# Attention rewritten as two passes over the scores, with two heads on the two halves of the TensorE array

## The chip, the cores and the metric

The kernel runs on one core of one Trainium2 chip. The metric is device time in microseconds (us) for one execution; lower is better. The program is one launch with three stages: causal attention with a learned decay, a first feed-forward of 2048 hidden units, and a second, gated feed-forward of 1536 hidden units.

## The reference

```python
B, H, S, D = 4, 8, 576, 64
scores = (1.0 / np.sqrt(D)) * np.matmul(q, k.transpose(0, 1, 3, 2))
causal = np.triu(np.ones((S, S), dtype=bool), k=1)
cum = np.cumsum(np.maximum(s, 0.0), axis=-1)
bias = -(cum[:, :, :, None] - cum[:, :, None, :])
scores = np.where(causal, -1e9, scores + np.minimum(bias, 0.0))
scores = scores - np.max(scores, axis=-1, keepdims=True)
attn = np.exp(scores)
attn = attn / (np.sum(attn, axis=-1, keepdims=True) + 1e-09)
out = np.matmul(attn, v)
x = out.transpose(0, 2, 1, 3).reshape(B * S, H * D)      # 2304 tokens of 512
h = x @ w_in;  y = softplus(h) @ w_out                   # first feed-forward
xn = y / rms(y) * rms_g
out = (silu(xn @ w_gate) * (xn @ w_val)) @ w_out2        # second feed-forward
```

The weights arrive as 64-bit floats. A product of two numbers is formed from parts: `hi` is a number rounded to the short type fp32r, `lo` is what is left, and three products (hi·hi, hi·lo, lo·hi) are added up.

## The kernel before

**Attention.** The 32 heads are taken as 16 pairs of two heads of one batch. For a pair, `a_load` fetches q and k, `a_qt` transposes them on TensorE (PE, 12 transposes, L357), and `a_qh` and `a_ql` split them into `hl`, whose partitions 0 to 63 belong to the first head and 64 to 127 to the second. `a_qd` copies the parts of one head by DMA into a tile `sk` (L381, L382), so that one matmul contracts over 68 rows (four of them carry the bias) and a second over 128 rows (both mixed products stacked). `a_s` makes the scores with queries on partitions, in four blocks of 128, 256, 384 and 512 keys (L418, L419), and adds the causal mask by a bf16 product (L420). The last 64 queries of both heads share one tile (`a_s4`, L427 to L431). `a_m` takes the negative row maximum on VectorE (DVE, L436), `a_e` the exponential with that maximum as bias and the row sum as a by-product on ScalarE (ACT, L449), and `a_n` scales each row by one over its sum on GpSimd (POOL, L472). `a_t` transposes the result on PE, with 15 transposes for a head, ten of 128 rows (L504) and five of 64 (L501). Then `a_v0` multiplies the first 384 queries by v in full float32 (L530, 64 columns of weights), and `a_v1` the others from hi and lo parts (L539).

**What sets the order.** Every engine runs its own instructions in program order. In attention the table `OFF` gives each step of head n the place n + offset, and all steps are sorted by it. Twelve of the weight chunks are converted meanwhile (`CONV`, on ACT, DVE and POOL). SP issues all of these DMAs, one after another.

**After attention.** `m1_h` (L642 to L644) needs x, which attention has written to DRAM as `xT`. The first two of these, H0 and H1, are placed at the end of the attention order. ACT, DVE and POOL then turn h into `gh` and `gl` (`m1_abs` to `m1_gl`; in the first six steps `m1_gl` runs on POOL, L694), and `m1_y` needs both. The tiles of this stage lie where the pools of attention lay, and wait for their last readers.

Of the kernel before, what the change touches and what calls it, by code (L numbers as in the profile page):

```python
# [8 lines left out]
F32 = mybir.dt.float32  # L9
# [131 lines left out]
def attention_moe_kernel(ctx, tc, q, k, v, s, w_in, w_out, w_gate, w_val, w_out2, rms_g, out):  # L141
    nc = tc.nc
# [46 lines left out]
    mask64 = const.tile([P, 64], BF16, tag="mask64", name="mask64")  # L189
    bds = []  # L190
    ones = const.tile([P, P], F32R, tag="ones", name="ones")
    gcol = const.tile([P, KD], F32, tag="gcol", name="gcol")
    aug = dram.tile([NH, 4, 2, S], F32R, tag="aug", name="aug")
    aug4 = dram.tile([NH, 4, P + S], F32R, tag="aug4", name="aug4")
# [92 lines left out]
    st = {}  # L287

    def setup():
# [3 lines left out]
        for r in (slice(0, 64), slice(64, P)):  # L293
            nc.gpsimd.tensor_copy(out=mask64[r], in_=mask16[r, r])
        for i in range(2):
            bd = pools["stack"].tile([P, 2, P], F32R, tag=f"bd{i}", name=f"bd{i}", bufs=1)
            bds.append(bd)
            nc.gpsimd.memset(f32(bd), 0.0)
        nc.vector.memset(f32(ones), 1.0)

    def make_cum(cp):
# [6 lines left out]
        rows = cp.tile([NH, 4, 2, S], F32R, tag="rows", name="rows")  # L308
        for r, w in ((0, 0), (1, 1), (2, 0), (3, 1)):
            nc.gpsimd.memset(f32(rows[:, r, w]), 1.0)  # L310
        zero = cp.tile([NH, 4, 64], F32, tag="zero", name="zero")
        nc.gpsimd.memset(zero, 0.0)
        for hd in range(2):
            c = (1 - hd) * 64
            nc.gpsimd.dma_start(out=f32(aug4[hd::2, :, c:c + 64]), in_=zero[hd::2])
# [3 lines left out]
        hi, lo = rows[:, 0, 1], rows[:, 2, 1]  # L319
        nc.vector.tensor_copy(out=hi, in_=cum)  # L320
        nc.scalar.activation(out=rows[:, 1, 0], in_=f32(hi), func=AF.Copy, scale=-1.0)
        nc.vector.tensor_tensor(out=lo, in0=cum, in1=f32(hi), op=ALU.subtract)
        nc.vector.tensor_tensor(out=rows[:, 3, 0], in0=f32(hi), in1=cum, op=ALU.subtract)
        nc.sync.dma_start(out=f32(aug), in_=f32(rows))
        for hd in range(2):
            nc.sync.dma_start(out=f32(aug4[hd::2, :, hd * 64:hd * 64 + 64]), in_=f32(rows[hd::2, :, 0, 512:S]))
        nc.sync.dma_start(out=f32(aug4[:, :, P:P + S]), in_=f32(rows[:, :, 1]))
        nc.gpsimd.dma_start(out=gcol, in_=rms_g.rearrange("(a p) -> p a", p=P))

    def pair_bh(p):  # L330
        return p // HP, 2 * (p % HP)

# [8 lines left out]
    def a_loadv(p):  # L341
        b, h = pair_bh(p)
        t = pools["nat"].tile([P, NB, 2, D], F32, tag="vn", name="vn", bufs=3)
        for hd in range(2):
            nc.sync.dma_start(
                out=t[:, 0:4, hd, :],
                in_=v[b, h + hd, 0:512, :].rearrange("(c p) d -> p c d", p=P))
        nc.sync.dma_start(
            out=t[:, 4], in_=v[b, h:h + 2, 448:576, :].rearrange("h p d -> p h d"))
        st["vn", p] = t  # L350

    def a_qt(p, which):
        nat = st.pop((("qn", "kn")[which], p))
        t = ps_s("qkT"), ps_s("qkT")
# [8 lines left out]
    def a_qh(p, which):  # L363
        if which == 0:
            st["hl", p] = pools["split"].tile([P, 4, S], F32R, tag="hl", name="hl", bufs=2)
# [10 lines left out]
    def a_qd(n):  # L376
        p, hd = divmod(n, 2)
        hl = f32(st["hl", p])[hd * D:(hd + 1) * D]
        sk = pools["stack"].tile([P, 2, 2, 512], F32R, tag="sk", name="sk", bufs=3)
        for dst, src in ((sk[4:4 + D, 0], hl[:, 0:3:2]), (sk[0:D, 1], hl[:, 0:4:3]), (sk[D:P, 1], hl[:, 1:3])):  # L380
            nc.sync.dma_start(out=f32(dst), in_=src[:, :, 0:512])  # L381
        nc.sync.dma_start(out=f32(sk[0:4, 0]), in_=f32(aug[n][:, :, 0:512]))  # L382
        st["sk", n] = sk

    def a_qb(p):
        a8 = pools["stack"].tile([8, P + S], F32R, tag="a8", name="a8", bufs=2)
        nc.sync.dma_start(out=f32(a8), in_=f32(aug4[2 * p:2 * p + 2]).rearrange("h r n -> (h r) n"))
# [11 lines left out]
    def a_vl(p):
        vn, vs = st["vn", p], st["vs", p]  # L400
        nc.gpsimd.tensor_tensor(out=vs[:, :, 1:3, :], in0=vn, in1=f32(vs[:, :, 0:4:3, :]), op=ALU.subtract)

    BLK = ((0, 2, 3), (1,))
    COL = {0: 0, 2: 1, 3: 2, 1: 3}
    SOFF = {0: 0, 1: 0, 2: 128, 3: 0}
    EO = {0: 0, 1: 128, 2: 384, 3: 768}

    def a_s(n, half):
        sk = st["sk", n]
        for blk in BLK[half]:  # L410
            if blk == 2:
                t = st["s", n, 0]
            else:
                t = st["x1"][:, 0:256] if blk == 1 else ps_s("s")
            st["s", n, blk] = t
            c, w = SOFF[blk], B0[blk] + P
            o, i = t[:, c:c + w], slice(B0[blk], w)
            nc.tensor.matmul(o, sk[0:D + 4, 0, 0, i], sk[0:D + 4, 0, 1, 0:w], start=True, stop=False)  # L418
            nc.tensor.matmul(o, sk[:, 1, 0, i], sk[:, 1, 1, 0:w], start=False, stop=False)  # L419
            nc.tensor.matmul(t[:, c + w - P:c + w], ident16, mask16, start=False, stop=True)  # L420

    def a_s4(p):
        a8, bd, hl = st.pop(("a8", p)), bds[p % 2], st["hl", p]
        t = st["s4", p] = ps_s("s4")[:, 0:256], ps_s("s4")[:, 0:320]
        for o, j0, w in ((t[0], 0, 256), (t[1], 256, 320)):
            j = slice(j0, j0 + w)
            nc.tensor.matmul(o, a8[:, 0:P], a8[:, P + j0:P + j0 + w], start=True, stop=False)  # L427
            nc.tensor.matmul(o, bd[:, 0], hl[:, 2, j], start=False, stop=False)
            nc.tensor.matmul(o, bd[:, 0], hl[:, 3, j], start=False, stop=False)
            nc.tensor.matmul(o, bd[:, 1], hl[:, 2, j], start=False, stop=(j0 == 0))  # L430
        nc.tensor.matmul(t[1][:, 256:320], ident16, mask64, start=False, stop=True)  # L431

    def a_m(n, blk):
        w = B0[blk] + P
        m = st["m", n, blk] = pools["sml"].tile([P, 1], F32, tag=f"m{blk}", name="m")
        nc.vector.reduce_max(out=m, in_=st["s", n, blk][:, SOFF[blk]:SOFF[blk] + w], axis=AX.X, negate=True)  # L436

    def a_m4(p):
        m = st["m4", p] = pools["sml"].tile([P, 2], F32, tag="m4", name="m4", bufs=2)
        for i, t in enumerate(st["s4", p]):  # L440
            nc.vector.reduce_max(out=m[:, i:i + 1], in_=t, axis=AX.X, negate=True)
        nc.vector.tensor_tensor(out=m[:, 0:1], in0=m[:, 0:1], in1=m[:, 1:2], op=ALU.min)

    def a_e(n, blk):
        if blk == 0:
            st["e", n] = pools["e"].tile([P, 1280], F32, tag="e", name="e")
            st["z", n] = pools["sml"].tile([P, 4], F32, tag="z", name="z")
        w, c = B0[blk] + P, COL[blk]
        nc.scalar.activation(out=st["e", n][:, EO[blk]:EO[blk] + w], in_=st["s", n, blk][:, SOFF[blk]:SOFF[blk] + w],  # L449
                             func=AF.Exp, bias=st.pop(("m", n, blk)), accum_out=st["z", n][:, c:c + 1])  # L450

    def a_e4(p):
        e = st["e4", p] = pools["e"].tile([P, S], F32, tag="e4", name="e4", bufs=2)
        z = st["z4", p] = pools["sml"].tile([P, 2], F32, tag="z4", name="z4", bufs=2)
        m = st.pop(("m4", p))
        for i, (t, c) in enumerate(zip(st.pop(("s4", p)), (slice(0, 256), slice(256, S)))):
            nc.scalar.activation(out=e[:, c], in_=t, func=AF.Exp, bias=m[:, 0:1], accum_out=z[:, i:i + 1])

    def a_r(n):
        r = st["r", n] = pools["sml"].tile([P, 4], F32, tag="r", name="r")  # L460
        z = st["z", n]
        nc.vector.tensor_scalar(out=z, in0=z, scalar1=1e-9, scalar2=None, op0=ALU.add)
        nc.vector.reciprocal(out=r, in_=z)

    def a_r4(p):
# [5 lines left out]
    def scale_rows(e, r):  # L471
        nc.gpsimd.tensor_scalar(out=e, in0=e, scalar1=r, scalar2=1.0, op0=ALU.mult, op1=ALU.mult)  # L472
# [484 lines left out]
```

## Time and profile before

| what | value |
|---|---|
| time, median of 2 runs | 1242.48 us (1240.45 to 1244.51) |
| the profiled execution, first to last instruction | 1242.4 us |
| PE busy | 1176.2 us (95%) |
| DVE, ACT, POOL busy | 771.7, 617.7, 471.5 us |
| first score matmul of attention | at 18.42 us |
| first h of the first feed-forward | at 314.62 us |
| first y of the first feed-forward | at 326.15 us |

A row of the timeline gives the start, the length, the engine, the line of the kernel, the operation, what it writes and reads, its shape, and how often it is repeated (x6); a bracket names idle time before it and what ended it. The length of a matmul includes its way through the array, so the pace of PE is read from the difference between the starts of neighbouring rows.

### The profile page before, as it was taken

How to read it: one execution, taken by the hardware profiler on the slowest of the kernel's cores; microseconds unless marked ns; L12 is line 12 of the kernel's file. 1: busy time of each engine (PE TensorE's matmuls, PEld its weight loads, DVE VectorE, ACT ScalarE, POOL GpSimd, SP SyncE). 2: the span in 40 equal slices, each digit the busy share in tenths (PEclk: the TensorE clock that was granted, in tenths of full speed). 3: DMA queues.
4: the chain of work that ended last, by engine and by line, in shares of the span. 5: the costliest groups of instructions: out<-in, count | busy, mean ns of one | idle time of the engine just before them, and what ended most of it. 6: DMA issues, size and time to landing. Idle time of an engine off the chain costs nothing.

```text
span 1242.4 us, 18308 instructions
## 1 busy us (share of the span) xinstructions
PE 1176.2 (95%) x6404; PEld 1042.1 (84%) x6404; DVE 771.7 (62%) x1396; ACT 617.7 (50%) x1467; POOL 471.5 (38%) x487
## 2 busy tenths in 40 slices
PE   4999999999999998999989879999999999999998
PEld 3677777776988888999888768899999999999997
DVE  4666676654699999998999999533333332333322
ACT  2667666665677777866666666442121121212111
POOL 4455655543354544346576776762000000000000
PEclk9999999999899998999999999999999999999999
DMA  9998888753333343544452332331101010010000
GB/s 181 198 192 178 200 193 186 167 131 100 99 129 119 122 139 123 162 140 134 159 165 91 120 101 85 117 97 58 39 14 39 14 39 1 14 39 13 26 1 26
DMA packets 139037, 128.96 MB, mean 104 GB/s; under 512 B 66656, under 2 KB 116352, under 8 KB 138912
## 3 DMA queue, kind: packets, MB, share of 16 engines
q1 hardware_dynamic: 138848, 127.74, 38.6%
q8 instruction: 51, 0.84, 0.3%
q14 instruction: 42, 0.34, 0.1%
q0 software_dynamic: 96, 0.04, 0.0%
HBM read 76.46 MB, written 26.12 MB: 83 GB/s over the span
## 4 chain that ended last, share of the span: by engine, by line
PE 67%; DVE 22%; ACT 4%; issue 3%; DMA 2%; SPq 2%; POOL 1%; DVEq 0%; POOLq 0%; ACTq 0%
DVE gl L694 5%; PE x L539 4%; PE pt L504 4%; PE g L644 4%; PE g L643 4%; PE v L644 4%; PE v L643 4%; PE v L642 4%; PE g L642 4%; PE o L530 4%; DVE l L685 4%; DVE e L677 3%; PE o L818 3%; PE o L819 3%; PE o L817 3%
## 5 line engine op out<-in xcount | busy, mean ns | idle before, releaser
L643 PE MATMUL y<-gl,w 128*128 128x384 f32 x384 | 134.5, 350 | 25.4 <-DVE gl L694 24.1
L252 POOL TENSOR_TENSOR wf<-ur 128x512 int32<-128x512 int32 x68 | 94.3, 1386 | 123.7 <-DVE ur L246 34.1
L802 DVE TENSOR_TENSOR u<-g,u 128x384 f32<-128x384 f32 x71 | 39.5, 556 | 158.9 <-ACT u L801 158.9
L642 PE MATMUL y<-gh,w 128*128 128x384 f32 x384 | 130.8, 341 | 3.1 <-ACT l L669 1.4
L644 PE MATMUL y<-gh,w 128*128 128x384 f32 x384 | 130.6, 340 | 0.0
L472 POOL TENSOR_SCALAR e<-e,r 128x256 f32<-128x256 f32 (+2 forms) x144 | 78.3, 560 | 127.9 <-ACT hl L368 103.1
L804 ACT ACTIVATE gh<-l 128x384 fp32r<-128x384 f32 x72 | 37.8, 524 | 156.0 <-DVE l L803 156.0
L801 ACT ACTIVATE u<-g 128x384 f32<-128x384 f32 x71 | 34.8, 490 | 151.9 <-PE g L644 151.8
L643 PEld LDWEIGHTS y<-gl,w 128*128 128x128 f32 x384 | 73.3, 191 | 36.7 <-DVE gl L694 35.1
L643 PE MATMUL g<-xl,w 128*128 128x384 f32 x284 | 95.6, 336 | 1.8 <-DVE xl L636 1.8
L689 ACT ACTIVATE gh<-l 128x384 fp32r<-128x384 f32 x96 | 49.9, 520 | 93.7 <-DVE l L685 93.5
L642 PE MATMUL g<-xh,w 128*128 128x384 f32 x284 | 95.8, 337 | 0.7 <-ACT xh L635 0.7
L694 DVE TENSOR_TENSOR gl<-l,gh 128x384 fp32r<-128x384 f32 x90 | 93.1, 1035 | 4.5 <-ACT gh L689 0.7
L644 PE MATMUL g<-xh,w 128*128 128x384 f32 x284 | 95.9, 338 | 0.0
L642 PE MATMUL h<-xh,w 128*128 128x384 f32 x256 | 89.2, 348 | 6.8 <-DVE e L681 6.6
L642 PE MATMUL v<-xh,w 128*128 128x384 f32 x284 | 94.9, 334 | 0.0
L644 PE MATMUL v<-xh,w 128*128 128x384 f32 x284 | 94.9, 334 | 0.0
L643 PE MATMUL v<-xl,w 128*128 128x384 f32 x284 | 94.9, 334 | 0.0
L643 PE MATMUL h<-xl,w 128*128 128x384 f32 x256 | 88.4, 345 | 3.5 <-POOL xl L639 3.3
L644 PE MATMUL h<-xh,w 128*128 128x384 f32 x256 | 87.4, 341 | 0.0
L685 DVE TENSOR_TENSOR l<-l,e 128x384 f32<-128x384 f32 x96 | 84.0, 875 | 3.7
L677 DVE SCALAR_TENSOR_TENSOR e<-u,e 128x384 f32<-128x384 f32 x96 | 73.9, 770 | 17.1 <-ACT l L669 17.1
(191 smaller groups left out, 3281.7 us busy)
## 6 DMA issues: line engine op xcount, KB each, us to landing
sk<-hl SPq DMA_DIRECT2D x96, 256.0 KB
raw<-in_moe_w_out_dram SPq DMA_DIRECT2D x28, 512.0 KB
raw<-in_moe_w_in_dram SPq DMA_DIRECT2D x16, 512.0 KB
raw<-in_moe_w_gate_dram SPq DMA_DIRECT2D x12, 512.0 KB
raw<-in_moe_w_val_dram SPq DMA_DIRECT2D x12, 512.0 KB
wf<-wf SPq DMA_DIRECT2D x24, 256.0 KB
wl<-wf SPq DMA_DIRECT2D x24, 256.0 KB
xr<-x SPq DMA_DIRECT2D x28, 192.0 KB
```

The lines of the kernel that those rows point to most:

```text
L252: nc.gpsimd.tensor_tensor(out=w.bitcast(I32), in0=u, in1=r3, op=ALU.add)
L472: nc.gpsimd.tensor_scalar(out=e, in0=e, scalar1=r, scalar2=1.0, op0=ALU.mult, op1=ALU.mult)
L504: nc.tensor.transpose(t[:, o:o + P], e[:, EO[ib] + j0:EO[ib] + j0 + P], ident)
L530: nc.tensor.matmul(o[:, IS - w:IS], vn[:, jb, hd, :], x[:, c:c + w], start=(jb == 0), stop=(jb == 2))
L539: nc.tensor.matmul(t[:, 192 - w:192], vs[r, jb, 2 * hd:2 * hd + 2, :].rearrange("p a d -> p (a d)"), x[r, c:c + w], start=(i == 0 and jb = ...
L642: nc.tensor.matmul(o, wh, xh, start=start, stop=False)
L643: nc.tensor.matmul(o, wh, xl, start=False, stop=False)
L644: nc.tensor.matmul(o, wl, xh, start=False, stop=stop)
L677: nc.vector.scalar_tensor_tensor(out=e, in0=st.pop(("u", i)), scalar=-1.0, in1=e, op0=ALU.add, op1=ALU.subtract)
L685: nc.vector.tensor_tensor(out=l, in0=l, in1=st.pop(("e", i)), op=ALU.add)
L689: nc.scalar.activation(out=gh, in_=st["l", i], func=AF.Copy)
L694: eng.tensor_tensor(out=gl, in0=st.pop(("l", i)), in1=f32(st["gh", i]), op=ALU.subtract)
```

## The change

Attention is rewritten; the feed-forward stages keep their code.

- **Pass one** (`a_one`) makes the scores of a pair from the hi parts alone, queries on partitions. For each block there are two matmuls a head: one over 40 rows (`aq` and `all`, which hold the bias rows of eight pairs, with `a_aq` picking one pair's), one over the 64 rows of `hl`. The heads alternate: the first uses partitions 0 to 63, the second 64 to 127, each with its own PSUM bank. The copies into `sk` are gone.
- `a_m` takes the row maxima (DVE), `a_mt` transposes them (PE), `a_mh` rounds them (ACT), and `a_md` sends them by four DMAs as a further row into `aq`.
- **Pass two** (`a_two`) makes the scores again, with keys on partitions and from all parts, four matmuls for each block and head; the maximum is subtracted inside the product. `a_e` takes the exponential. No transposes of it follow.
- `a_v` multiplies by `vn`, which has a block of ones between the two heads' values, in full float32 with 128 columns of weights: 64 rows of the result are the values, 64 the row sums.
- The sum goes by DMA into a tile of 9 columns (`a_zd`), is inverted (`a_zr`), goes to DRAM (`a_rd`) and back, spread over 64 partitions (`a_rb`); `a_xm` multiplies on POOL, `a_xw` writes x.
- The order is made by `attention_order`, which gives each step an engine, a duration, what it waits for and a priority, and takes the step that can start first.

The diff, cut to its core (PSUM tags: four banks `s`, two `p`, one each `o0` and `x1`):

```diff
+        for i in range(3):
+            t = pools["nat"].tile([P, NB, 3, D], F32, tag=f"vn{i}", name=f"vn{i}", bufs=1)
+            nc.gpsimd.memset(t[:, :, 1, :], 1.0)
+            nc.gpsimd.memset(t[0:64, 4], 0.0)
+        for g in range(2):
+            for w in range(2):
+                t = pools["stack"].tile([P, S], F32R, tag=f"all{g}{w}", name=f"all{g}{w}", bufs=1)
+                for r in (slice(32, 64), slice(96, P)):
+                    nc.gpsimd.memset(f32(t[r]), float(w))
...
+    ONE = {
+        "A": ((0, 0, 0, 128, 1), (128, 256, 0, 384, 1)),
+        "B": ((0, 384, 0, 512, 1),),
+        "C": ((0, 128, 0, 256, 1), (256, 448, 320, 256, 1)),
+        "D": ((0, 448, 0, 320, 0),),
+    }
+    TWO = {
+        "a": ((0, 0, 0, 448, 128),),
+        "b": ((0, 0, 448, 128, 0), (128, 384, 384, 192, 128), (320, 448, 512, 64, 64)),
+        "c": ((0, 128, 128, 448, 128),),
+        "d": ((0, 256, 256, 320, 128),),
+    }
+    def a_one(p, banks, last):
...
+                for a in range(2):
+                    for hd in range(2):
...
+                        if a == 0:
+                            r = slice(64 * hd, 64 * hd + MR)
+                            x, y = aq[r, ii], al[r, jj]
+                        else:
+                            x, y = hl[r, 0, ii], hl[r, 2, jj]
+                        nc.tensor.matmul(t[hd][:, c:c + w], x, y, start=(n == 0 and a == 0),
...
+                nc.tensor.matmul(t[hd][:, c:c + P], ident16, mask16, start=False, stop=True, skip_group_check=True)
+    def a_md(p):
...
+            nc.sync.dma_start(out=aq[r, 0:512], in_=mt[4 * hd:4 * hd + 4])
+            nc.sync.dma_start(out=aq[r, 512:S], in_=mt[8 + hd:9 + hd, 64:P])
+    def a_two(p, banks, last):
...
+                for a, (x, y) in enumerate(((None, None), (2, 0), (2, 1), (3, 0))):
+                    for hd in range(2):
...
+    def a_v(p, hd, part):
...
+            jobs = ((0, 0, 0, 384), (1, 832, 128, 256), (2, 1280, 256, 128))
...
+            jobs = ((0, 384, 0, 192), (3, 576, 0, 192), (4, 768, 128, 64), (1, 1088, 0, 192), (2, 1408, 0, 192))
+        for n, (jb, c, oc, w) in enumerate(jobs):
+            nc.tensor.matmul(o[:, oc:oc + w], vn[:, jb, hd:hd + 2].rearrange("p a d -> p (a d)"), e[:, c:c + w],
...
+    def a_zd(p):
+            nc.sync.dma_start(out=z[half(hd)], in_=st["xz", p, hd][64 - 64 * hd:65 - 64 * hd, :])
+    def a_rd(p):
+        nc.sync.dma_start(out=rdd[p].rearrange("h (p c) -> (h p) c", c=9), in_=st.pop(("z", p)))
+    def a_rb(p):
+            nc.sync.dma_start(out=rb[half(hd)], in_=rdd[p][hd:hd + 1].broadcast_to([64, S]))
+    def a_xm(p):
+            nc.gpsimd.tensor_tensor(out=x[r], in0=st.pop(("xz", p, hd))[r], in1=rb[r], op=ALU.mult)
...
```

PE, in the middle of attention. Before, one head's larger score blocks (`s`), a mask, and the transposes of an earlier head's rows (`pt`):

```order
L418 MATMUL s<-sk 128x384
L419 MATMUL s<-sk 128x384
L420 LDWEIGHTS ident_76
L420 MATMUL s<-mask_77,ident_76 128x128
L418 MATMUL s<-sk 128x512
L419 MATMUL s<-sk 128x512
L420 LDWEIGHTS ident_76
L420 MATMUL s<-mask_77,ident_76 128x128
L504 MATMUL pt<-ident,e 128x128 x6
```

Now, at such a place, the last block of pass one (`s`) and the first two banks of pass two of another pair (`t`); x2 is one matmul for each head, x6 three:

```order
L434 MATMUL s<-all_162,aq 128x320 x2
L434 MATMUL s<-hl 128x320 x2
L492 MATMUL t<-aq,all_162 128x448 x2
L492 MATMUL t<-hl 128x448 x6
L492 MATMUL t<-aq,all_162 128x128 x2
L492 MATMUL t<-hl 128x128 x6
L492 MATMUL t<-aq,all_162 128x192 x2
L492 MATMUL t<-hl 128x192 x6
L492 MATMUL t<-aq,all_162 128x64 x2
L492 MATMUL t<-hl 128x64 x6
L499 LDWEIGHTS mask_77
L499 MATMUL t<-ident_76,mask_77 128x128
```

The transposes are gone, and runs of half-height matmuls of the two heads stand in the place of full-height ones; the masks come together behind them.

POOL, at the start of the program. Before, between the masks and the bias rows (`rows`):

```order
L294 COPY mask64_78<-mask16_77 64x64 x2
L298 MEMSET bd0_133 128x256
L298 MEMSET bd1_135 128x256
L310 MEMSET rows_154 32x576 x4
```

Now, at that place, after two rows each for `vn0` and `vn1` that read like those for `vn2`:

```order
L302 MEMSET vn2_150 128x5x64
L303 MEMSET vn2_150 64x192
L309 MEMSET all00_153 32x576 x2
L309 MEMSET all01_156 32x576 x2
L309 MEMSET all10_159 32x576 x2
L309 MEMSET all11_162 32x576 x2
L313 MEMSET mc0_165 128x128
L313 MEMSET mc1_167 128x128
L329 MEMSET rows_190 32x576 x4
```

The filling of `vn`, `all` and `mc` has come ahead of `rows`, which the first bias DMAs wait for.

POOL, at the end of attention, now; `x<-xz,rb` is `a_xm`, two for each pair, and `gl` the first feed-forward's:

```order
L399 TENSOR_SCALAR aq<-all_159,oh 128x576
L551 TENSOR_TENSOR x<-xz,rb 64x576 x10
L769 TENSOR_TENSOR gl<-l,gh 128x384
L714 TENSOR_TENSOR xl<-xr,xh 128x384
L769 TENSOR_TENSOR gl<-l,gh 128x384
```

The last pair's multiplication by its inverted sums stands ahead of the first `gl`.

## Rows read from the trace of the kernel before

**Rows 1.** The span, from the page of the profile.
```profile
span 1242.4 us, 18308 instructions
```

**Rows 2.** A stretch of attention by engine: busy us (instructions), granted clock, DMA share, GB/s.
```profile
120.00:160.00 40.00, 40.00 (x246) 28.42 (x244) 28.26 (x78) 26.95 (x85) 20.58 (x29) 1.00 0.84 194
```

**Rows 3.** PE's timeline, from one pair's first score matmul to the next pair's.
```profile
154.14 0.33 PE L418 MATMUL s<-sk 68*128 68x128 f32 x1
...
155.26 0.40 PE L419 MATMUL s<-sk 128*128 128x512 f32 x1
155.50 0.23 PE L420 MATMUL s<-mask,ident 128*128 128x128 bf16 x1
155.57 0.83 PE L504 MATMUL pt<-ident,e 128*128 128x128 f32 x6
156.15 0.36 PE L418 MATMUL x<-sk 68*128 68x256 f32 x1
...
156.54 0.67 PE L357 MATMUL qkT<-ident,qn 96*128 96x96 f32 x6
157.05 0.27 PE L504 MATMUL pt<-ident,e 128*128 128x128 f32 x1
157.25 0.27 PE L501 MATMUL pt<-ident,e 64*128 64x64 f32 x1
157.45 0.33 PE L504 MATMUL pt<-ident,e 128*128 128x128 f32 x1
...
157.98 1.51 PE L530 MATMUL o<-p,vn 128*64 128x384 f32 x6
159.42 0.33 PE L504 MATMUL pt<-ident,e 128*128 128x128 f32 x1
...
165.06 0.28 PE L429 MATMUL s<-hl,bd 128*128 128x256 f32 x1
165.17 0.28 PE L430 MATMUL s<-hl,bd 128*128 128x256 f32 x1
...
165.97 0.31 PE L429 MATMUL s<-hl,bd 128*128 128x320 f32 x1
166.12 0.31 PE L430 MATMUL s<-hl,bd 128*128 128x320 f32 x1
...
171.82 0.33 PE L418 MATMUL s<-sk 68*128 68x128 f32 x1
```

**Rows 4.** Groups by line and shape, up to 400 us: busy us, mean ns of one.
```profile
L436 DVE TENSOR_REDUCE m<-s 128x1 f32<-128x512 f32 x32 | 21.8, 682 | 1.3 <-PE s L420 1.3
...
L401 POOL TENSOR_TENSOR vs<-vn,vs 128x640 fp32r<-128x640 f32 x16 | 24.7, 1546 | 1.3
```

**Rows 5.** The timeline of the start, all engines.
```profile
0.74 0.40 SPq L303 DMA_DIRECT2D sv<-in_s_dram  x1
...
2.67 0.53 DVE L316 TENSOR_SCALAR sv<-sv 32x576 f32<-32x576 f32 x1 [1.08 <-DMA sv<-in_s_dram]
...
3.65 2.45 POOL L310 MEMSET rows<- 32x576 f32 x4
...
14.25 1.39 SPq L382 DMA_DIRECT2D sk<-aug  x1
...
18.42 0.45 PE L418 MATMUL s<-sk 68*128 68x128 f32 x1 [8.58 <-DMA sk<-aug]
...
28.14 0.67 PE L418 MATMUL s<-sk 68*128 68x384 f32 x1
...
28.61 0.52 PE L419 MATMUL s<-sk 128*128 128x384 f32 x1
```

**Rows 6.** The timeline where the first feed-forward begins.
```profile
314.62 0.69 PE L642 MATMUL h<-xh,w 128*128 128x384 f32 x1
...
322.63 0.56 DVE L685 TENSOR_TENSOR l<-l,e 128x384 f32<-128x384 f32 x1
...
326.15 0.33 PE L642 MATMUL y<-gh,w 128*128 128x384 f32 x1
```

More of the change, by code (lines that the diff above doesn't have):

```diff
@@ L188, in attention_moe_kernel @@
     mask16 = const.tile([P, P], BF16, tag="mask16", name="mask16")
[L189 to L190 removed]
+    oh32 = const.tile([P, 32], F32, tag="oh32", name="oh32")
+    oh = const.tile([P, 8], F32, tag="oh", name="oh")
+    vns, mcs, alls = [], [], {}
     ones = const.tile([P, P], F32R, tag="ones", name="ones")
     gcol = const.tile([P, KD], F32, tag="gcol", name="gcol")
[L193 to L194 removed]
+    aug = dram.tile([2, 2, NH // 2, 4, S], F32R, tag="aug", name="aug")
+    rdd = [dram.tile([2, S], F32, tag=f"rd{p}", name=f"rd{p}") for p in range(NP)]
     xT = [dram.tile([DM, S], F32, tag=f"x{b}", name=f"x{b}") for b in range(B)]
@@ L307, in make_cum @@
         nc.vector.memset(one, 1.0)
-        rows = cp.tile([NH, 4, 2, S], F32R, tag="rows", name="rows")
+        rows = cp.tile([NH, 2, 4, S], F32R, tag="rows", name="rows")
         for r, w in ((0, 0), (1, 1), (2, 0), (3, 1)):
[L310 to L315, printed above, removed]
+            nc.gpsimd.memset(f32(rows[:, w, r]), 1.0)
         nc.vector.tensor_scalar(out=sv, in0=sv, scalar1=0.0, scalar2=None, op0=ALU.max)
@@ L399, in a_vl @@
[L399 to L442, printed above, removed]
@@ L523, in a_v0 @@
-    def a_v0(n):
-        p, hd = divmod(n, 2)
-        if hd == 0:
-            st["o0", p] = ps_1("o0")
-        o = st["o0", p][hd * D:(hd + 1) * D]
-        vn, x = st["vn", p], st["p0", n]
-        for jb, (c, w) in enumerate(((0, 384), (384, 256), (640, 128))):
-            nc.tensor.matmul(o[:, IS - w:IS], vn[:, jb, hd, :], x[:, c:c + w], start=(jb == 0), stop=(jb == 2))
-    def a_v1(n):
-        p, hd = divmod(n, 2)
-        vs = st["vs", p]
-        t = st["o1", n] = st["x1"][:, 256:448]
-        for i, x in enumerate((st["ph", n], st["pl", n])):
-            for jb, c in ((0, 0), (1, 192), (2, 448), (3, 640), (4, 384)):
-                r, w = (slice(0, P), 192) if jb < 4 else (slice(64, P), 64)
-                nc.tensor.matmul(t[:, 192 - w:192], vs[r, jb, 2 * hd:2 * hd + 2, :].rearrange("p a d -> p (a d)"),
-                                 x[r, c:c + w], start=(i == 0 and jb == 0), stop=(i == 1 and jb == NB - 1))
@@ L542, in halves @@
-    def halves(hd):
-        return (slice(0, 64), slice(64, P)) if hd == 0 else (slice(64, P), slice(0, 64))
-    def a_ox(p):
-        st["x", p] = pools["xo"].tile([P, IS], F32, tag="x", name="x")
-        nc.scalar.activation(out=st["x", p], in_=st.pop(("o0", p))[:, 0:IS], func=AF.Copy)
-    def a_oc(n):
-        a, b_ = halves(n % 2)
-        tmp = pools["xo"].tile([P, S - IS], F32, tag="tmp", name="tmp", bufs=2)
-        nc.scalar.activation(out=tmp[a], in_=st["o1", n][b_, 0:S - IS], func=AF.Copy)
-        st["tmp", n] = tmp
@@ L594, in attention_moe_kernel, with a_aq @@
-    CONV = {"CF": w_fetch, "CA": w_conv_a, "CD": w_conv_d, "CP": w_conv_p, "CH": w_hi, "CL": w_lo}
-    TAIL = {
-        "XL": lambda: x_load0(),
-        **{f"X{a}": (lambda a=a: x_split(0, a, nc.vector)) for a in range(KD)},
-        "H0": lambda: m1_h(0), "H1": lambda: m1_h(1),
-    }
+    def a_aq(p):
+        aq = st["aq", p] = pools["stack"].tile([P, S], F32R, tag="aq", name="aq", bufs=3)
+        c = p % G8
+        nc.gpsimd.tensor_scalar(out=aq, in0=f32(alls[p // G8, 0]), scalar1=oh[:, c:c + 1], scalar2=1.0,
+                                op0=ALU.mult, op1=ALU.mult)
@@ new lines, in attention_moe_kernel @@
+    ONE_PS = {"A": "s", "B": "s", "C": "p", "D": "p"}
+    def a_one(p, banks, last):
+        aq, al, hl = st["aq", p], alls[p // G8, 1], st["hl", p]
+        masks = st.setdefault(("one", p), [])
+        for bk in banks:
+            t = [(ps_s if ONE_PS[bk] == "s" else ps_p)("s") for _ in range(2)]
+            st["s", p, bk] = t
+            for n, (c, i, j, w, diag) in enumerate(ONE[bk]):
+                for a in range(2):
+                    for hd in range(2):
+                        r, ii, jj = half(hd), slice(i, i + P), slice(j, j + w)
+                        if a == 0:
[4 more added lines that the diff above has]
+                        nc.tensor.matmul(t[hd][:, c:c + w], x, y, start=(n == 0 and a == 0),
+                                         stop=(a == 1 and not diag), skip_group_check=True)
+                if diag:
+                    masks.append((t, c + w - P))
+        while last and masks:
+            t, c = masks.pop(0)
+            for hd in range(2):
+                nc.tensor.matmul(t[hd][:, c:c + P], ident16, mask16, start=False, stop=True, skip_group_check=True)
@@ new lines, in a_m @@
+    def a_m(p, bk, hd):
+        m, t = mcs[p % 2], st["s", p, bk][hd]
+        c = 4 * hd
+        if bk == "A":
+            outs = ((m[:, c:c + 1], t[:, 0:128]), (m[:, c + 2:c + 3], t[:, 128:512]))
+        elif bk == "B":
+            outs = ((m[:, c + 3:c + 4], t),)
+        elif bk == "C":
+            outs = ((m[:, c + 1:17 + hd:15 - 3 * hd], t.rearrange("p (n j) -> p n j", n=2)),)
+        else:
+            outs = ((m[:, 8 + hd:9 + hd], t[:, 0:320]),)
+        for o, x in outs:
+            nc.vector.reduce_max(out=o, in_=x, axis=AX.X, negate=True)
@@ new lines, in a_mn, with a_mt, a_mh @@
+    def a_mn(p):
+        m = mcs[p % 2]
+        nc.vector.tensor_tensor(out=m[:, 8:10], in0=m[:, 8:10], in1=m[:, 16:18], op=ALU.min)
+    def a_mt(p):
+        st["mT", p] = ps_p("mT")
+        nc.tensor.transpose(st["mT", p][:, 0:P], mcs[p % 2], ident)
+    def a_mh(p):
+        mt = st["mt", p] = pools["sml"].tile([16, P], F32R, tag="mt", name="mt", bufs=2)
+        nc.scalar.activation(out=mt, in_=st.pop(("mT", p))[0:16, 0:P], func=AF.Copy)
+    def a_md(p):
+        mt, aq = f32(st.pop(("mt", p))), f32(st["aq", p])
+        for hd in range(2):
+            r = slice(64 * hd + MR, 64 * hd + MR + 1)
+            nc.sync.dma_start(out=aq[r, 0:512], in_=mt[4 * hd:4 * hd + 4])
+            nc.sync.dma_start(out=aq[r, 512:S], in_=mt[8 + hd:9 + hd, 64:P])
@@ new lines, in a_two @@
+    def a_two(p, banks, last):
+        aq, al, hl = st["aq", p], alls[p // G8, 1], st["hl", p]
+        masks = st.setdefault(("two", p), [])
+        for bk in banks:
+            t = [ps_s("t") for _ in range(2)]
+            st["t", p, bk] = t
+            for n, (c, j, i, w, diag) in enumerate(TWO[bk]):
+                jj, ii = slice(j, j + P), slice(i, i + w)
+                for a, (x, y) in enumerate(((None, None), (2, 0), (2, 1), (3, 0))):
+                    for hd in range(2):
+                        r = half(hd)
+                        if a == 0:
+                            r = slice(64 * hd, 64 * hd + MR + 1)
+                            lt, rt = al[r, jj], aq[r, ii]
+                        else:
+                            lt, rt = hl[r, x, jj], hl[r, y, ii]
+                        nc.tensor.matmul(t[hd][:, c:c + w], lt, rt, start=(n == 0 and a == 0),
+                                         stop=(a == 3 and not diag), skip_group_check=True)
+                if diag:
+                    masks.append((t, c, diag))
+        while last and masks:
+            t, c, w = masks.pop(0)
+            for hd in range(2):
+                nc.tensor.matmul(t[hd][:, c:c + w], mask16, ident16[:, P - w:P], start=False, stop=True,
+                                 skip_group_check=True)
@@ new lines, in a_e @@
+    def a_e(p, bk, hd):
+        if bk == "a":
+            st["e", p, hd] = pools["e"].tile([P, 1600], F32, tag="e", name="e")
+        c, w = EO[bk]
+        nc.scalar.activation(out=st["e", p, hd][:, c:c + w], in_=st["t", p, bk][hd][:, 0:w], func=AF.Exp)
+    def a_v(p, hd, part):
+        vn, e = vns[p % 3], st["e", p, hd]
+        if part == 0:
+            o = st["o", p, hd, 0] = ps_1("o0")
+            jobs = ((0, 0, 0, 384), (1, 832, 128, 256), (2, 1280, 256, 128))
+        else:
+            o = st["o", p, hd, 1] = ps_1("x1")
+            jobs = ((0, 384, 0, 192), (3, 576, 0, 192), (4, 768, 128, 64), (1, 1088, 0, 192), (2, 1408, 0, 192))
+        for n, (jb, c, oc, w) in enumerate(jobs):
+            nc.tensor.matmul(o[:, oc:oc + w], vn[:, jb, hd:hd + 2].rearrange("p a d -> p (a d)"), e[:, c:c + w],
+                             start=(n == 0), stop=(n == len(jobs) - 1))
@@ new lines, in attention_moe_kernel, with a_ox @@
+    IS = 384
+    def a_ox(p, hd, part):
+        if part == 0:
+            st["xz", p, hd] = pools["xo"].tile([P, S], F32, tag="xz", name="xz", bufs=4)
+        c = (slice(0, IS), slice(IS, S))[part]
+        nc.scalar.activation(out=st["xz", p, hd][:, c], in_=st.pop(("o", p, hd, part))[:, 0:c.stop - c.start], func=AF.Copy)
+    def a_zd(p):
+        z = st["z", p] = pools["sml"].tile([P, 9], F32, tag="z", name="z", bufs=2)
+        for hd in range(2):
+            nc.sync.dma_start(out=z[half(hd)], in_=st["xz", p, hd][64 - 64 * hd:65 - 64 * hd, :])
@@ new lines, in a_zr @@
+    def a_zr(p):
+        z = st["z", p]
+        nc.vector.tensor_scalar(out=z, in0=z, scalar1=1e-9, scalar2=None, op0=ALU.add)
+        nc.vector.reciprocal(out=z, in_=z)
+    def a_rd(p):
+        nc.sync.dma_start(out=rdd[p].rearrange("h (p c) -> (h p) c", c=9), in_=st.pop(("z", p)))
+    def a_rb(p):
+        rb = st["rb", p] = pools["xo"].tile([P, S], F32, tag="rb", name="rb", bufs=2)
+        for hd in range(2):
+            nc.sync.dma_start(out=rb[half(hd)], in_=rdd[p][hd:hd + 1].broadcast_to([64, S]))
```

304 lines of the change are left out of this document (152 added, 152 removed).

## The prediction

> **What bounds the kernel now.** I read the page first: the profiled execution spans 1242.4 us [rows 1], and the median of the two runs is 1242.48, so nothing has to be added to a sum made against the span. Then the busy time by stretch: in the middle of attention PE is busy for all of 40 us, while DVE, ACT and POOL stand at 28, 27 and 21 [rows 2]. So attention is bound by PE. What PE spends there is read from the starts in its timeline: one pair takes 171.82 - 154.14 = 17.68 us [rows 3], 16 pairs 283 us. Attention's last product ends where the first h begins, at 314.62, and the first y starts at 326.15 [rows 6]. All that comes after keeps its code and its order; so the change is worth what it moves this first y, and the time is 1242.4 plus that shift.
>
> **The pace of PE.** One fp32r matmul that follows another of the same shape takes 0.24 us at 512 columns, 0.15 at 320 and 0.11 at 256 [rows 3], or 0.47 ns a column; that gives 0.18 at 384 and 0.21 at 448. Narrower ones I price at 0.11 too, since the load of their weights remains. Six transposes alike take 0.58 us, 0.10 each; but between 128 rows and 64 rows each takes 0.20 (157.05, 157.25, 157.45), so a change of array height costs about 0.10.
>
> **A pair after the change.**
> - Scores, pass one: the widths 128, 384, 512, 256, 256, 320, two matmuls each and head: 2 x (0.11 + 0.18 + 0.24 + 0.11 + 0.11 + 0.15) = 1.8 us for one head.
> - Scores, pass two: 448, 128, 192, 64, 448, 320, four each: 4 x (0.21 + 3 x 0.11 + 0.21 + 0.15) = 3.6 us for one head.
> - If the two heads, on different halves of the array and in different banks, run together, these 5.4 us serve the pair; if not, it is 10.8. No row of before has two neighbours on different halves. Below 5.4 nothing can go, since the columns must be streamed. I take 5.4: the row nearest to the question is the cost of changing the height, which arises where one tile overlaps the rows of the next, and here the tiles share neither rows, nor weights, nor banks.
> - The Trainium skill, "TensorE: Matmul & The Clock Gate", section "The mechanism" (Part 3), says that matmuls on different row groups run at the same time, and that a weight load overlaps a running matmul only where the row group differs. By it the two heads cost 5.4; no run here shows it yet.
> - Values: six instructions for 768 columns of full float32 take 159.42 - 157.98 = 1.44 us [rows 3], 1.88 ns a column. The new products have 1600 columns a head: 6.0 us a pair. That stretch ends with a change of shape, which I count apart; without it 5.6. I take 5.8. The weights are 128 columns wide instead of 64; the load is hidden behind two passes of 64 to 384 columns, and if it is not, 6.0 is nearer.
> - Transposes of q and k, unchanged: 157.05 - 156.54 = 0.51 for six, 1.0 a pair. Masks: 20 instead of 9, at 155.57 - 155.50 = 0.07: 1.4. Transpose of the maxima: 0.1.
> - Changes of array height: the order has 166 up to the first y, 10.4 a pair: 1.0.
> - Sum: 5.4 + 5.8 + 1.0 + 1.4 + 0.1 + 1.0 = 14.7 us. PE now waits in order for maxima and exponentials, which it does not before; I allow 0.25 (none at best; the other end is the third rival). So **14.95** instead of 17.68. The 15 transposes and 10 value products from parts of each head are gone.
>
> **The other engines.** DVE spends 28.3 of 40 us, 12.5 a pair. It loses the lo parts of the transposed rows and the sums over halves. Its maxima, one a block and head, are those of 3712 columns: with 0.68 us for 512 [rows 4] some 5 us, near what it spends now. ACT loses four copies a head for two and keeps its exponentials. POOL loses the scaling of rows and gains two products of 64 x 576; 640 columns take 1.55 us [rows 4], so 2.8. All of these stay under 13, behind PE's 14.95. SP issues about as many DMAs as before, 18 a pair, and loses those into `sk`. Nothing of this is charged; what a late one of them would cost is the third rival.
>
> **The start.** POOL fills 576 columns in 2.45 / 4 = 0.61 us [rows 5]. The new fillings, 1536 columns of `vn`, eight of 576 and the two `mc`, come to 6.8 us, those removed to about 0.6; `rows` is then ready at 12.3, not 6.1. A DMA is issued in 0.4 to 1.4 us, and lands 1.5 (1.14 to 2.67) to 2.8 us (15.64 to 18.42) after that [rows 5]; I use 0.5 and 2. Bias to DRAM, four back into `all`, and one selection on POOL: 12.3 + 2.5 + 4 + 0.7 = about 20 us for the first score matmul (18.42 now). Its maxima end 7 us later, DVE's other work adds some 3, transpose, rounding and four DMAs 5: the first pass two starts at **35**. By then PE has done the transposes and pass one of two pairs, about 8 us of work. PE's early rows are at the lower level of its clock: 384 columns take 28.61 - 28.14 = 0.47 us [rows 5]. I put 6 us for as much again here.
>
> **The end.** H0 and H1 (24 matmuls at 0.18) cost 4.3 us within attention; the last pair, with no neighbour to fill its waits for exponentials, 4. So the last value product ends at 35 + (16 x 14.95 - 8) + 4.3 + 6 + 4 = 280.5. Then the last pair's sums travel: copies on ACT 0.8, three DMA trips of 2.5 with two issues twice, 8.5, inverse 0.3, two products on POOL 2.8, some 13 us in all. POOL's first `gl` stands behind that, and tiles of the first feed-forward lie on those that are read there. From DVE's sum to y it is 326.15 - 322.63 = 3.5 [rows 6]. Two more h are the only work of PE that can run meanwhile. First y: 280.5 + 13 + 3.5 = **297**, 29 us before 326.15. Time: 1242.4 - 29 = **1213 us**. The bounds: a pair of 14.2 to 15.9 moves it by 12 to 15 us either way, DMA trips at 1.9 or 4.2 by 2 and 5.
>
> **The rivals.**
> - *The weights of the two halves are loaded in turn* (the columns still together). A pair of matmuls then takes at least 2 x 0.11 = 0.22: 36 of these come to 8.1 us, 2.7 more for each pair of heads, 43 us: 1256. For it: in the rows a matmul of 256 columns or fewer is at 0.11 already. Against it: nothing but the argument above.
> - *The halves do not run together at all.* 10.8 instead of 5.4: 86 us more, 1299, slower. It decides from a pair of 14.95 + 29 / 16 = 16.8 us on; over 2% slower from 18.4. For it: no row shows two matmuls at once. Against it: the order, which puts the heads in turn into different banks.
> - *The banks, not PE, set the pace.* Each pair goes three times through the four banks `s`, and a mask at the end of each round keeps DVE and ACT from starting early. Four reads of 0.6 to 0.7 us empty a round; two of them, 1.3 us, must end before PE can begin the next. If PE finds nothing else to do in two rounds of three, that is 2.3 us a pair beyond what I allow, some 37 us in all: 1250. Against it: 8 us of other PE work a pair. The Trainium skill, "TensorEngine Tiling (Array Packing)", section "PSUM Bottleneck", says that tiling speeds up TensorE but not the emptying of PSUM; in before, with PE busy throughout, no row shows such a wait.
>
> **How the numbers follow.** My forecast has 0.60, with its own range 1195 to 1230; the banks 0.18, the weights in turn 0.14, no overlap 0.08. The range 1194 to 1252 holds nearly all of the first two and a part of the third. Over 2% (about what a measurement of this kernel can tell from no change) means under 1217.6 or over 1267.3. Faster: four fifths of the forecast and a little of the banks, 0.50. Slower: no overlap and a tail of the weights, 0.09. The rest, 0.41, is within 2%.
>
> **What would show it.** In the changed profile: neighbouring starts of the two heads' matmuls near 0 and 0.2 apart in turn (not 0.11 or 0.2 evenly); a pair every 15 us in mid-attention; PE's waits there short; the first pass two near 35 us; the last value product near 280; and a first y some 16 us behind it, with POOL's `gl` waiting for `x<-xz,rb`. I would be wrong by most if PE's waits for banks or for the DMAs of maxima came to more than 1 us a pair, if the clock fell in attention, or if the halves ran apart.

## The result, and the profile after

The changed kernel takes 1258.82 us (median of two runs, 1258.26 to 1259.38) against 1242.48: a ratio of 1.013, 95% interval 1.0085 to 1.0171. The prediction was 1213 us (1194 to 1252): the time lies outside its range, and the sign is wrong. The profiled execution spans 1257.6 us and is the one read here.

The page's span, and the windows of mid-attention (busy us and instructions of PE, its weight loads, DVE, ACT and POOL, then granted clock, DMA share, GB/s), against [rows 1, 2]:

```profile
span 1257.6 us, 18473 instructions
```
```profile
60.00:100.00 40.00, 36.77 (x283) 30.02 (x280) 17.07 (x43) 14.27 (x37) 11.68 (x11) 0.83 0.45 102
120.00:160.00 40.00, 37.88 (x298) 30.28 (x296) 18.18 (x46) 15.08 (x40) 14.85 (x13) 0.90 0.43 110
160.00:200.00 40.00, 37.47 (x305) 29.87 (x305) 16.96 (x41) 16.24 (x43) 16.21 (x14) 1.00 0.31 85
```

DVE, ACT and POOL fell to 17, 16 and 16 us of 40, as planned. But PE, which was never idle there before, now stands still for 2 to 3 us of 40, and its clock is at its lower level (1.2 GHz) for a part of two of the three stretches. A part of the waiting hides within the busy time, as PE's timeline of a pair shows (start, us, engine, line, operation, tile; in brackets the idle time before and its releaser), against [rows 3]:

```profile
168.83 0.46 PE L492 MATMUL t<-aq,all 41*128 41x448 f32 x1
169.48 0.44 PE L492 MATMUL t<-aq,all 41*128 41x448 f32 x1 [0.19 <-DVE mc L455]
169.49 1.05 PE L492 MATMUL t<-hl 64*128 64x448 f32 x6
170.21 0.75 PE L492 MATMUL t<-aq,all 41*128 41x128 f32 x2
...
173.61 0.78 PE L377 MATMUL qkT<-ident,qn 96*128 96x96 f32 x6 [0.58 <-DVE mc L455]
174.32 0.47 PE L492 MATMUL t<-aq,all 41*128 41x448 f32 x2
174.63 0.78 PE L492 MATMUL t<-hl 64*128 64x448 f32 x6
175.25 0.31 PE L492 MATMUL t<-aq,all 41*128 41x320 f32 x2
```

At 168.83 the first head's matmul starts; the second head's needs the other bank, which DVE's maxima still read, and comes at 169.48. The same block a little later, with both banks free, takes 0.93 us (174.32 to 175.25), with the two heads starting 3 to 4 ns apart. PE's longest waits from 60 to 300 us (us in total, times, longest) name whom it waits for:

```profile
PE qkT L377 <- DVE mc L455: 7.0, 9, 2.4
PE t L492 <- DVE mc L455: 3.0, 13, 0.3
PE s L434 <- ACT e L506: 1.8, 4, 0.4
```

The first and largest of them is not for the four banks `s`: the transposes of q and k (`qkT`) go into the two banks `p`, which pass one's third and fourth blocks use too, and wait for the maxima of those blocks. Pass two (`t`) and pass one's first two blocks (`s`) wait for the banks `s`.

DVE itself is not short of time, it gets its work in lumps. Its timeline around 200 us:

```profile
199.34 0.82 DVE L393 SCALAR_TENSOR_TENSOR hl<-qkT,hl 128x384 fp32r<-128x384 f32 x2 [6.31 <-ACT hl L388]
202.17 3.81 DVE L455 TENSOR_REDUCE mc<-s 128x2 f32<-128x512 f32 x8 [2.01 <-PE s L441]
```

It is idle for 6.3 and 2.0 us while PE computes the values of a pair in one piece, then all of pass one arrives, and PE waits behind eight maxima. The pair's pace: the first value product of a pair starts at 46.8 for the first pair and at 306.7 for the fifteenth, 18.56 us apart on average, against 14.95 predicted and 17.68 before. Three pairs in a row lie in a stretch at full clock, from one first value product (141.87) to the third after it (193.75):

```profile
141.87:193.75 51.88, 47.82 (x414) 38.03 (x413) 25.15 (x61) 20.25 (x53) 16.53 (x15) 1.00 0.41 106
```

They take 17.3 us each, and PE stands idle for 1.35 us of that; so a pair is 2.3 us over the forecast with the clock never at its lower level.

At the ends, against [rows 5, 6], PE's first score matmul, its first of pass two, then the last value products and the chain from POOL through ACT to y:

```profile
18.23 0.47 PE L434 MATMUL s<-all,aq 40*128 40x128 f32 x2 [9.11 <-POOL aq L399]
...
36.58 0.74 PE L492 MATMUL t<-aq,all 41*128 41x448 f32 x2
```
```profile
322.43 1.69 PE L517 MATMUL x<-e,vn 128*128 128x192 f32 x10
...
332.76 2.86 POOL L551 TENSOR_TENSOR x<-xz,rb 64x576 f32<-64x576 f32 x2 [10.05 <-DMA rb<-rd]
...
335.66 0.49 ACT L736 ACTIVATE e<-h 128x384 f32<-128x384 f32 x1 [11.17 <-POOL x L551]
...
342.99 0.50 PE L717 MATMUL y<-gh,w 128*128 128x384 f32 x1
```

The first y comes at 342.99, 16.8 us after that of before; from there to the end it is 914.6 us (916.2 before).

### The profile page after: what moved, and what is told of

Read it like the earlier page. It is cut to its first block, busy times and chain, and to the rows that moved or that the text cites. A ratio compares the mean times of both kernels' runs of the same rounds, so it can differ in the third digit from the quotient of the medians.

```text
span 1257.6 us, 18473 instructions
## 1 busy us (share of the span) xinstructions
PE 1161.6 (92%) x6884; PEld 1056.0 (84%) x6884; DVE 721.1 (57%) x1208; ACT 545.9 (43%) x1179; POOL 420.6 (33%) x368
## 4 chain that ended last, share of the span: by engine, by line
PE 44%; DVE 21%; ACT 3%; issue 2%; DMA 1%; POOL 1%; DVEq 0%
DVE gl L769 5%; PE g L719 4%; PE g L718 4%; PE v L718 4%; PE v L719 4%; PE v L717 4%; PE g L717 4%; DVE l L760 4%; DVE e L752 3%; PE o L893 3%; PE o L894 3%; PE o L892 3%; DVE e L756 2%; DVE ur L243 2%; DVE ur L247 2%
## 5 line engine op out<-in xcount | busy, mean ns | idle before, releaser
L455 DVE TENSOR_REDUCE mc<-s 128x1 f32<-128x384 f32 (+4 forms) x160 | 75.2, 536 | 67.9 <-PE s L441 57.0
L506 ACT ACTIVATE e<-t 128x448 f32<-128x448 f32 (+2 forms) x128 | 54.1, 509 | 108.2 <-PE t L499 108.2
## 6 DMA issues: line engine op xcount, KB each, us to landing
xr<-x SPq DMA_DIRECT2D x28, 192.0 KB
```

The costliest lines, as they stand in the source:

```text
L455: nc.vector.reduce_max(out=o, in_=x, axis=AX.X, negate=True)
L506: nc.scalar.activation(out=st["e", p, hd][:, c:c + w], in_=st["t", p, bk][hd][:, 0:w], func=AF.Exp)
```

## The experiments

Two theories. **Waits**: PE's work for a pair is about what was forecast, and 3 us a pair are waits for PSUM banks, laid down by the order of the steps. **Work**: the halves gain less than forecast, or the clock is the cause, and PE is simply slower.

**Shorter maxima.** The maxima read only the last 128 keys of a block (64 in the fourth), so they are not the true maxima:

```diff
-            outs = ((m[:, c + 3:c + 4], t),)
+            outs = ((m[:, c + 3:c + 4], t[:, 384:512]),)
```


> The row maxima are taken over the last 128 keys of each block only (64 of the fourth), so the maximum is not that of the whole row; DVE needs 2.9 us a pair for them instead of 5.3, everything else and the order stay. If waits for the banks that DVE empties hold PE up: 15 to 35 us less, 1224 to 1243. If the half-rate clock or the DMA of the maxima is what holds PE up: within 6 us of 1258.


Measured 1228.59, ratio 0.989 (0.9839 to 0.9945): 30 us under the change, with PE's program untouched. A lump of eight maxima, 3.81 us in the change, and the window of mid-attention are now:

```profile
181.82 1.94 DVE L455 TENSOR_REDUCE mc<-s 128x2 f32<-128x256 f32 x8 [2.02 <-PE s L441]
```
```profile
160.00:200.00 40.00, 38.88 (x353) 32.09 (x352) 12.09 (x43) 15.68 (x42) 11.90 (x11) 1.00 0.40 101
```

A pair took 16.5 us, and from 36 us to the last value product (291.6) the clock did not fall. So PE waited for the maxima.

**No row of maxima.** The four DMAs that bring a pair's maxima into `aq` are left out.


> The four DMAs a pair that send the maxima into the weights of pass two are left out, so no maximum is subtracted; the maxima are still taken, transposed and rounded. If the way of the maxima (SP's queue and the landing) holds pass two up: 30 us less or more, under 1228. If the banks do: 0 to 10 us less, 1248 to 1258, and PE's waits stay where they are.


Measured 1258.16, ratio 1.013 (1.008 to 1.0179): no change. So the transfers of the maxima do not hold PE up.

**The halves apart.** In each bank all of the first head's matmuls stand ahead of the second's, in the order of the change and, later, in the new order told below (shown for pass two; pass one alike):

```diff
-                for a, (x, y) in enumerate(((None, None), (2, 0), (2, 1), (3, 0))):
-                    for hd in range(2):
+            for hd in range(2):
+                for n, (c, j, i, w, diag) in enumerate(TWO[bk]):
+                    jj, ii = slice(j, j + P), slice(i, i + w)
```


> In both passes all matmuls of the first head of a bank are issued before those of the second, so the two halves of the array hardly ever have work at the same time; all results stay the same. If PE's own work sets the pace of a pair (18.1 us), the 5.4 us of scores become 10.8 and the time rises by 86 us, to about 1345. If PE stands some 3 to 4 us a pair in waits that the order leaves, a part of the 5.4 us falls into them: 35 to 65 us more, 1294 to 1324. If the halves had not run together in the changed kernel either, no change.

> The new order, with the two halves of the array kept apart as in the earlier run (first head of a bank, then second). If the new order lets PE set the pace, the overlap is now worth nearly all of its 5.4 us a pair: 60 to 86 us more than the new order alone, where the old order lost 24. If other engines set the pace: again 25 or less.


Measured 1282.36 (24 us over the change, but its two runs lie 13 us apart, 1275.91 and 1288.81) and 1254.40 (25.5 over the new order). The first is between the theories. The second is about what was expected if other engines set the pace, but it doesn't show that, since PE's timeline shows that this edit hardly parts the halves:

```profile
170.01 0.48 PE L493 MATMUL t<-aq,all 41*128 41x448 f32 x2
170.32 0.78 PE L493 MATMUL t<-hl 64*128 64x448 f32 x6
171.03 0.72 PE L377 MATMUL qkT<-ident,kn 96*128 96x96 f32 x6
171.67 0.33 PE L493 MATMUL t<-aq,all 41*128 41x128 f32 x1
171.84 0.49 PE L493 MATMUL t<-hl 64*128 64x128 f32 x3
172.17 0.30 PE L493 MATMUL t<-aq,all 41*128 41x192 f32 x1
172.32 0.49 PE L493 MATMUL t<-hl 64*128 64x192 f32 x3
172.65 0.33 PE L493 MATMUL t<-aq,all 41*128 41x64 f32 x2
172.70 0.61 PE L493 MATMUL t<-hl 64*128 64x64 f32 x6
```

In the bank of 448 columns the two matmuls over `aq` still start together (x2 at 170.01), though the second head's is the fifth in the program. In the next bank the first head runs alone through eight matmuls, and with its ninth (172.65) the second head's first starts, the thirteenth of the program (the x2 counts its 128 columns under the shape of the ninth). In both banks, then, a matmul for the idle half of the array started four places ahead of its turn. Where a bank has four matmuls a head, the two heads still ran together; only the bank with twelve a head was slowed much.

**Both heads on one half.** In the new order, the second head's scores are computed from the first head's rows (those of `aq` and `all` too):

```diff
-                        r = half(hd)
+                        r = half(0)
```


> What two halves are worth, which the two kernels with the halves apart did not show: their traces have the second head's matmuls starting up to four places ahead of their turn, beside the first head's, so the overlap was hardly taken away. Here, in the replanned order, both heads' scores are computed from the first head's rows, on one half of the array, with the same instructions in the same order; the second head's scores are the first's (a part of the computation that is left out for the time). Theory that the halves overlap: the score matmuls of a pair (7.7 us in blocks with two heads side by side) take some 5 to 6 us more, a pair some 20.5 to 21.5 in place of 15.5, 16 pairs 80 to 95 us: 1310 to 1325. Rival (PE is not what bounds a pair, or the two heads never gained by lying side by side): under 1260.


Measured 1381.20 us, ratio 1.111 (1.1071 to 1.1148): 152 us over the new order, 9.5 a pair, more than the 80 to 95 expected. Its windows:

```profile
140.00:180.00 40.00, 40.00 (x222) 32.24 (x222) 14.66 (x37) 11.12 (x29) 10.20 (x9) 0.86 0.30 81
180.00:220.00 40.00, 40.00 (x216) 33.28 (x215) 10.02 (x25) 10.86 (x29) 7.41 (x7) 0.79 0.23 59
```

A block of eight matmuls of 448 columns at full clock, up to the start of what follows it, in the new order and then on one half:

```profile
164.99 0.37 PE L492 MATMUL t<-aq,all 41*128 41x448 f32 x2
...
165.91 0.33 PE L463 MATMUL mT<-ident,mc 128*128 128x128 f32 x1
```
```profile
189.33 0.57 PE L492 MATMUL t<-aq,all 41*128 41x448 f32 x2
...
191.05 0.33 PE L463 MATMUL mT<-ident,mc 128*128 128x128 f32 x1
```

It took 1.72 us in place of 0.92, one of 256 columns 1.15 in place of 0.68; summed over a pair's score blocks (the one of 512, never at full clock, in proportion) that is 5.3 us, as the prediction had it (5.4). The other 4.2 go with the clock: PE is busy throughout and hardly waits (0.2 us from 60 to 350), yet the granted clock is 0.79 to 0.86, where the same instructions on both halves had 1.00. It falls behind stretches of scores on one half (scores from 179.7 to 185.0, lower level from 185.2; scores from 188.6, lower level from 192.0).

**The new order.** Nothing but the planner: the durations that its steps have on the chip (2.4 us for a transfer), and new places within a pair for each kind of step, found by a search on a model of the planner. With the places come a longer look-ahead, a few more dependencies, and a wider spacing of the twelve weight conversions.

```diff
+            dur = DUR.get(name[0], DUR.get(name[0][:2], dur))
+            lat = 2.4 if name[0] in ("DM", "ZD", "RS", "BC") else lat
+                prio = name[1] * PER + PRIO[nm] + (int(name[0][2]) if nm[0] == "E" else 0)
```


> Only the order of attention's steps changes: the planner gets the durations read from the changed kernel's trace and other offsets, found by trying many until PE's steps stood close together; every step and its result stay. If the waits of the order are what holds PE up: a pair comes down from 18.1 us to 14.1 (PE's own work) to 15.5, the last value product from 324.6 to some 275 to 285, and the time to 1205 to 1220, where the forecast was. If PE's own work or the half-rate clock costs the 18.1: no more than 15 us less.


Measured 1228.89, ratio 0.989 (0.9864 to 0.9912): 30 us under the change with the same instructions. The windows:

```profile
120.00:160.00 40.00, 40.00 (x347) 31.52 (x345) 22.77 (x53) 17.51 (x44) 13.26 (x12) 1.00 0.40 104
160.00:200.00 40.00, 40.00 (x371) 31.78 (x367) 22.20 (x46) 18.89 (x49) 17.09 (x15) 1.00 0.38 93
```

PE is busy throughout, at full clock from 62 to 304 us, and a pair takes 15.5 us. In the change the four parts of a pair's values run together (193.7 to 200.3 us of its trace) and all score rounds after them; here they stand in three places (169.1; 172.1 and 173.6; 178.4) with score rounds between, so that DVE and ACT empty banks while PE computes values. The time is 9 us above the 1205 to 1220 expected: pass two begins at 43.55, 7 us later than in the change, and the last value product ends at 297.0, not by 285.

**The new order with short maxima.**


> The new order, with the maxima over the last 128 keys of each block alone, as in the earlier run. If the new order leaves no waits for DVE, nothing more is gained, 0 to 6 us; if DVE still holds the banks, 15 to 30 as in the old order.


Measured 1228.85, no change: in this order shorter maxima gain nothing, so they no longer hold PE up.

**Its two parts alone.** Durations without the new places, and places (with what comes with them) without the durations; the 2.4 us of a transfer stands in both.


> The changed kernel with the measured durations in its planner's table (what an instruction takes on the chip, and 2.4 us for a transfer) and its own priorities otherwise: does the plan err by wrong durations or by the places it aims for? If durations were at fault: pairs of 15.5 to 16 and 1228 to 1240. If the order of a pair (the places aimed for) is at fault, and the durations matter little: 1250 to 1265.

> The counterpart of the kernel with the durations only: the replanned kernel's places (the offset that each kind of step aims for within a pair), with the planner's durations as the change has them, but for the 2.4 us of a transfer. The durations alone gave nothing (1258.5). If the places alone carry the gain, the plan's slightly wrong durations are harmless: 1226 to 1236, pairs of 15.5 to 16. If the places need the durations they were searched with (a plan that walks by wrong times picks other steps): 1240 to 1260, pairs over 16.5 and waits of PE for maxima.


Durations only: 1258.51, no gain; windows with PE at 37.3 and 37.7 of 40 as in the change. Places only: 1238.53, ratio 0.996 (0.9937 to 0.9978), pairs of 15.5 to 15.6. So the places carry the pace, and the rest of the gain, 10 us by the medians, comes only with both (in the profiled executions, 5 us apart, the first y stands at 319.98 against 314.67). Which part of the new places does it, the steps' offsets or what comes with them, was not tried.

**The last pair's sums.** In the change's order the last pair is not divided at all (POOL copies it):


> For the last pair alone the sums are not sent, inverted and spread; its values are copied by POOL instead and stay undivided. If the way of the last sums holds the first y back (18.4 us from the last value product to it): the first y comes 8 to 10 us earlier against the last value product, and the time falls by as much, to about 1250. If reused tiles or the clock hold it back: under 3 us.


Measured 1247.52, ratio 1.003 (1.0004 to 1.0062): 11 us under the change, with the first y 6.7 us behind the last value product in place of 18.9. Then in the new order the sums are inverted without DMA, first by DVE's reciprocal, then by ACT:

```diff
+                nc.scalar.activation(out=rb[half(hd)], in_=st["xz", p, hd][half(1 - hd)], func=AF.Ln)
+                nc.scalar.activation(out=rb[half(hd)], in_=rb[half(hd)], func=AF.Exp, scale=-1.0)
```


> The new order, and for the last pair alone the sums are moved to the values' partitions by ACT, inverted and multiplied on DVE, instead of three DMA trips and POOL; all results stay. The gap from the last value product to the first y, 18.4 us in the changed kernel, falls to 7 to 11, and the time is 7 to 11 us below that of the new order alone. If the gap is due to other things, under 3.

> The replanned order, with one thing more: the last pair's sums go through no DMA and no POOL. ACT takes the logarithm of the 64 rows of sums that lie on the other half and then exp of its negative (two instructions of 64x576 a head), and DVE multiplies (two instructions). Its first try, with the reciprocal on DVE, gained nothing since one reciprocal of 64x576 took 3.75 us. Chain theory: after the last copy of the sums (297.4 in the replanned kernel) four instructions of some 0.7 us on ACT and two of 0.77 on DVE end at about 301.5, so that ACT's first read of h in the feed-forward comes at about 301.5 in place of 306.95: 1222 to 1225, some 5 us under the replanned order. Rival (the boundary is set by something else, the first weights or h itself): no change from 1229.


With the reciprocal: 1231.24, ratio 0.991 (0.9883 to 0.9931), no gain over the new order. Its timeline on DVE:

```profile
298.31 0.45 DVE L540 TENSOR_SCALAR rb<-rb 64x576 f32<-64x576 f32 x1 [4.14 <-ACT rb L539]
298.80 3.75 DVE L541 RECIPROCAL rb<-rb 64x576 f32<-64x576 f32 x1
```

One reciprocal of 576 columns takes 3.75 us, and there are two. With the logarithm and exp on ACT, 0.68 each: **1224.73**, ratio 0.985 (0.9826 to 0.9875), 1.5% under the kernel before. ACT's first read of h comes at 301.37, as expected, in place of 306.95:

```profile
300.18 0.68 ACT L540 ACTIVATE rb<-rb 64x576 f32<-64x576 f32 x1
301.37 0.49 ACT L770 ACTIVATE e<-h 128x384 f32<-128x384 f32 x1 [0.50 <-DVE x L564]
```

## Why the prediction was wrong

- **The step that failed** is the 0.25 us a pair for PE's waits. The change runs at 18.56 us a pair, 3.6 over the forecast of 14.95. The new order, in which PE hardly waits, runs the same instructions at 15.5, so the 14.7 for PE's own work was at most 0.8 low. The other 3.0 us, where 0.25 was allowed, are waits and clock: 42 us over the 14 pairs between the first and the fifteenth. The first y was missed by 46 (342.99 against 297).
- The third rival, **the banks set the pace**, came nearest to the mechanism: it asked for two rounds of three without other work and priced that at 2.3 us a pair beyond the forecast. The "8 us of other PE work a pair" held against it is there, but the order puts its largest piece, the values, ahead of the rounds, where it covers none of them. The order was given; its steps had only to be read against the banks. The rival looked at the four banks `s` alone; the largest wait that the trace names is for the two banks `p`, which it left out. The section "PSUM Bottleneck" of the Trainium skill's "TensorEngine Tiling (Array Packing)", cited for that rival, agrees with these rows in part: with the halves together, the emptying of the banks held PE up in the change (short maxima gained 30 us), but not in the new order (they gained nothing).
- **The clock** was named as what would make the prediction wrong, and not priced but for 6 us at the start. It stands at its lower level for 37.5 us between 60 and 320 us. Of the 3.0 us a pair, 1.8 are there without it (the three pairs at full clock, 17.3 against 15.5); so some 1.2 are left for the clock, an estimate. That is within what 37.5 us at half the clock can cost, 19 us, or 1.3 a pair. The kernel with the durations only has 27 us of the lower level in that time and the same total. Why the clock fell in the change stays open; it did not in the new order, nor with short maxima.
- **The halves overlap**, as forecast: starts 3 to 4 ns apart, 5.3 us a pair when taken away at full clock. The rivals "weights in turn" (whose 36 pairs at 0.22 come to 7.9 us, not 8.1) and "no overlap" fall. The Trainium skill's rule, cited from "TensorE: Matmul & The Clock Gate", section "The mechanism" (Part 3), that matmuls on different row groups run at once, agrees with that.
- **The other engines** were right: the maxima are 5.1 us a pair (5 forecast), and none comes near PE. But "all of these stay under 13" says nothing of when they run, and it was used as if it did.
- **The start** was right: 18.2 (20 forecast) and 36.6 (35). The 0.47 us that it read as the pace at the lower clock also holds a change from 68 to 128 rows; the next 384 columns of before took 0.32 (28.61 to 28.93). **The end** was nearly so: 18.9 us from the last value product (324.1) to y, 16.5 forecast. POOL's products end at 335.6, 11.5 us after it (13 forecast); but what waits for them is ACT's first read of h, 7.3 us ahead of y, not DVE's sum, 3.5 ahead.

## What to carry to other kernels

Busy shares per pair say who could be the bound; here, with engines that run a fixed order, it was decided by what stands between two uses of the same bank. Before trusting a sum, lay one period of the new order on each engine with its durations, and see whether the work that shall cover a bank's emptying stands between the rounds or ahead of them. If the instructions are right and the time is not, move the order before touching the instructions: here that was worth 30 us.

## What the runs showed of the hardware

- Matmuls for the idle half of the array started four places ahead of their turn in the program, in both banks looked at (170.01 and 172.65); parting the halves in the program did not part them in time where a head had four matmuls in a bank.
- TensorE's clock fell to its lower level with PE busy all the time, behind scores on one half of the array (0.79 and 0.86 granted in two stretches of 40 us); with the heads on both halves the same order ran at 1.00.
- DVE's reciprocal of 64x576 took 3.75 us, 6.5 ns a column, against 0.45 us for adding a constant to the same tile; Ln and Exp on ACT took 0.68 us each.
